# Pooled attention and two feed-forwards: the second output weight converted during the first feed-forward, and read back from DRAM

## The chip, the cores and the metric

One core of one Trainium2 chip. The metric is the device time of one execution in microseconds; of several executions the median is given. The profile is a trace of one execution. Its engines are TensorE (PE, with its weight loads as PEld), VectorE (DVE), ScalarE (ACT), GpSimd (POOL) and SyncE (SP); POOL and SP issue the transfers (DMA) between DRAM and the on-chip memory.

## What is computed

```python
k_p, v_p = k, v averaged over groups of 8 positions          # 576 -> 72
attn = softmax(q @ k_p.T / sqrt(64)) @ v_p                   # batch 8, 8 heads, 576 x 64
x = attn as 4608 tokens x 512
h = ((x @ w1) * (x @ w2)) @ w3                               # 512 -> 1024 -> 1024
x2 = h @ w_out                                               # 1024 -> 512
g = softplus(x2 @ w_in)                                      # 512 -> 2048
out = g @ w2_out                                             # 2048 -> 512, 4608 x 512
```

The attention inputs are 32-bit floats; the six weights arrive as 64-bit floats. `w2_out` (called `wo2_d` in the kernel, 2048 x 512) is the weight that the change is about.

## The kernel before

A 64-bit weight is loaded as pairs of 32-bit words and put together into 32-bit floats by one ACT operation and four DVE operations (`convert_1024`, lines 225 to 232: ABS of the upper word, a clamp, a shift, the sign, the lower word's top bits). Most matmuls take each operand as two numbers: hi, a copy rounded to the type that PE multiplies, and lo, what is left of it. The products hi·hi, hi·lo and lo·hi are summed (`mm3`, lines 122 to 124).

The program has two parts. In **the first**, 4608 tokens go in 9 blocks j of 512, and every block in 8 steps i (`p1_step`). A step multiplies x by 128 columns of w1 and of w2 (`ab`, 24 matmuls; ACT drains the first product at line 539, DVE multiplies at 542, ACT and DVE split the result at 117 and 118), and adds the step before to x2 (`x2_mm`, 12 matmuls). Attention for later tokens and weight conversions lie between the steps: `slot_1` calls `att_slot()` and then `bg(1)` or `bg(2)`, which runs one or two pieces of the generators in the list `background`. The last of these is `left_factors`, which converts `w_in`, forms the factors of a 7-product (Strassen-like) scheme and stores them in DRAM as hi and lo (`wis`), one of 8 tiles after another. x2 goes to DRAM too (`x2d`).

In **the second part**, 6 sweeps s of 768 tokens pass over 8 steps t each, so 48 steps n. A step makes 7 products (`product`, 42 matmuls of 384 columns into X and Z), with ACT draining at lines 802, 814, 820 and 837 and DVE adding at 807, 825 and 831. Softplus of the step before runs on ACT and DVE (`soft_ops`), and the step before that is multiplied by `w2_out` (`o_part`, 36 matmuls of 512 columns). The factors of a step come back from `wis` by DMAs that POOL issues (line 613), two a step, each after the product that reads its old place. Every engine runs its instructions in the order in which the code writes them.

`w2_out` is converted by `wo2_jobs`. Its places (tags `wgh0` to `wgl7`) are those of w1 and w2, so tile t can be written only when the last block no longer reads w1 and w2 there (`p1_done`). Tiles 0 to 3 are converted in pieces of 1024 columns during block j = 8, tiles 4 to 7 in pieces of 512 during steps 0 to 7 of the second part, by `bg(2)`, `bg(1)`, `bg(2)`, `bg(2)` in each step. The hi copy is line 640 (ACT), lo is 642 (DVE).

Of the kernel before, what the change touches and what calls it, by code (L numbers as in the profile page):

```python
# [8 lines left out]
F32 = mybir.dt.float32  # L9
F32R = mybir.dt.float32r  # L10
I32 = mybir.dt.int32
AF = mybir.ActivationFunctionType
# [36 lines left out]
def pooled_attention_two_ffn(ctx: ExitStack, tc: tile.TileContext, qT_d, kT_d, v_d, w12_d, w3T_d, wo_d, wi_d, wo2_d, out):  # L49
# [145 lines left out]


    background = []
    p1_done = set()

    def bg(steps):  # L200
        while steps and background:
# [21 lines left out]
    def convert_1024(raw, y):  # L223
        yi = y.bitcast(I32)
        nc.scalar.activation(y, raw[:, :, 1].bitcast(F32), AF.Abs, scale=HI_SCALE)
        yield
        nc.vector.tensor_scalar(y, y, HI_MIN, HI_MAX, op0=ALU.max, op1=ALU.min)
        nc.vector.tensor_scalar(yi, yi, 3, None, op0=ALU.logical_shift_left)
        yield
        nc.vector.scalar_tensor_tensor(yi, raw[:, :, 1], -0x80000000, yi, op0=ALU.bitwise_and, op1=ALU.bitwise_or)  # L230
        yield
        nc.vector.scalar_tensor_tensor(yi, raw[:, :, 0], 29, yi, op0=ALU.logical_shift_right, op1=ALU.bitwise_or)
        yield

    def left_factors():

        t2k_ring[0] = Ring([T2K + 8 + 2 * i for i in range(4)])
        stage = Ring([RAW + 8, RAW + 12])
        raw, y, S = mem(RAW, [P, 1024, 2], I32), mem(T2K, [P, 1024]), mem(T2K + 4, [P, 1024])
        for _ in range(8):  # L240
            yield
        nc.sync.dma_start(raw.rearrange("p n t -> p (n t)"), wi_d[0].rearrange("p q k f -> p (q k f)").bitcast(I32))
        yield
        for t in range(F8):
            yield from convert_1024(raw, y)
            if t + 1 < F8:
                nc.sync.dma_start(raw.rearrange("p n t -> p (n t)"), wi_d[t + 1].rearrange("p q k f -> p (q k f)").bitcast(I32))
            a11, a12, a22, a21 = (y[:, 256 * i:256 * i + 256] for i in range(4))
            s2, s3, s1, s4 = (S[:, 256 * i:256 * i + 256] for i in range(4))
            nc.vector.tensor_add(s1, a21, a22)  # L250
            nc.vector.tensor_sub(s3, a11, a21)
            yield
            nc.vector.tensor_sub(s2, s1, a11)
            nc.vector.tensor_sub(s4, a12, s2)
            yield
            w3_, w4_ = wis[t]
            for src, dsts in (
                (y[:, :512], [w3_[:, :, 0:2, :]]),
                (y[:, 512:768], [w4_[:, :, 2, :]]),
                (S[:, :512], [w3_[:, :, 2, :], w4_[:, :, 0, :]]),  # L260
                (S[:, 512:], [w4_[:, :, 1, :], w4_[:, :, 3, :]]),
            ):
                n = src.shape[1]
                st = stage([P, 2, 512])[:, :, :n]
                hi = st[:, 0, :].bitcast(F32R)
                nc.scalar.activation(hi, src, AF.Copy)
                yield
                nc.vector.tensor_sub(st[:, 1, :].bitcast(F32R), src, st[:, 0, :])
                n //= len(dsts)
                for i, dst in enumerate(dsts):  # L270
                    dst = dst.rearrange("p h c f -> p h (c f)") if len(dst.shape) == 4 else dst
                    nc.sync.dma_start(dst, st[:, :, n * i:n * i + n])
                yield


    ident = main.tile([P, P], F32, tag="ident", name="ident")
# [170 lines left out]
    with tc.manual_schedule():  # L447
# [115 lines left out]
        def p1_step(j, i, slots):  # L563
            st = ab(j, i)
            next(st)
            slots[0]()
            next(st)
            slots[1]()
            if (j, i) != (0, 0) and (j, i) <= (NB - 1, K1 // 2):
                x2_mm(*((j, i - 1) if i else (j - 1, K1 - 1)))  # L570
            slots[2]()
# [32 lines left out]

        c_ring = {0: Ring([0, 3]), 1: Ring([6])}
        e_ring, us = Ring([9, 12]), (mem(15, [P, TS]), mem(18, [P, TS]))
        o_ring = Ring([21, 23])
        wgroup = {}

        def load_factors(n, i):  # L610
# [3 lines left out]

        wo2_hl = {}

        def load_wo2(raw, t, parts):
            for n, i in enumerate(parts):
                f = t + F8 * i
                nc.sync.dma_start(raw[:, 512 * n:512 * n + 512, :].rearrange("p n t -> p (n t)"), wo2_d[f * P:f * P + P, :].bitcast(I32))  # L620

        def wo2_jobs(ts, ys, raws, parts):


            seq = [(t, p) for t in ts for p in parts]
            for n in range(min(len(raws), len(seq))):
                load_wo2(raws[n], *seq[n])
            for n, (t, p) in enumerate(seq):
                while (NB - 1, 2 * (t // 2) + 1) not in p1_done:
                    yield  # L630
                raw, y = raws[n % len(raws)], ys[n % len(ys)]
                yield from convert_1024(raw, y)
                if n + len(raws) < len(seq):
                    load_wo2(raw, *seq[n + len(raws)])
                if p[0] == 0:
                    w2 = [main.tile([P, 2, 512], F32R, tag=f"wg{x}{t}", name=f"w2{x}{t}") for x in "hl"]
                    for i in range(2):
                        wo2_hl[t + F8 * i] = w2[0][:, i, :], w2[1][:, i, :]
                hi, lo = (w[:, p[0]:p[-1] + 1, :].rearrange("p i f -> p (i f)") for w in w2)
                nc.scalar.activation(hi, y, AF.Copy)  # L640
                yield
                nc.vector.tensor_sub(lo, y, hi.bitcast(F32))
                yield


        xq_ring = Ring([XODD + 6 * i for i in range(8)] + [GBUF + 8])
# [40 lines left out]
        load_factors(1, 0)  # L687
        load_factors(1, 1)
        x2_load(0)
        background.append(wo2_jobs(range(4), [mem(T2K, [P, 1024]), mem(T2K + 4, [P, 1024])], [mem(RAW + 8 * i, [P, 1024, 2], I32) for i in range(2)], [(0, 1)]))  # L690

        for i in range(i7, K1):
            p1_step(NB - 2, i, [slot_1] * 3)
        xs = x2_steps(0)
        for i in range(K1):
            p1_step(NB - 1, i, [slot_1] * 3)
            p1_done.add((NB - 1, i))

            for _ in range((2, 1, 1, 0, 1, 1, 1, 0)[i]):
                next(xs)  # L700
        while background:
            bg(1)
        background.append(wo2_jobs(range(4, 8), [mem(25, [P, 512])], [mem(27, [P, 512, 2], I32)], [(0,), (1,)]))

        rest = [(i, ms) for i in range(K1 // 2, K1) for ms in ((0, 1), (2, 3))]

# [78 lines left out]
        for n in range(NH + 2):  # L785
            s, t = divmod(n, F8)
            h = n < NH
            if n == 2:

                o_ring = Ring([21, 23, 25, 27, 29])  # L790
            if h and t == 3 and s + 1 < NS:
                xs = x2_steps(s + 1)

            def factors(*when):

                if h and t in when and (s if t < 3 else s + 1) < NS:
                    next(xs, None)

            if h:
                soft[n, 0], soft[n, 1] = (c_ring[i]([P, TS]) for i in range(2))  # L800
                product(n, 0)
                nc.scalar.activation(snap[0], xz[0], AF.Copy)
            soft_step(n - 1, 0)
            soft_step(n - 1, 1)
            if h:
                product(n, 1)
                nc.vector.tensor_add(soft[n, 0][:, :HS], snap[0], xz[1])  # L807
            o_part(n - 2, 0, 0)
            factors(0, 7)
            soft_step(n - 1, 1)  # L810
            bg(2)
            if h:
                product(n, 2)
                nc.scalar.activation(snap[1], xz[0], AF.Copy)  # L814
            soft_step(n - 1, 0)
            o_part(n - 2, 0, 1)
            bg(1)
            if h:
                product(n, 3)
                nc.scalar.activation(snap[0], xz[1], AF.Copy)  # L820
            factors(0)
            soft_step(n - 1, 0)
            if h:
                product(n, 4)
                nc.vector.tensor_add(soft[n, 1][:, HS:], snap[0], xz[0])
            o_part(n - 2, 0, 2)
            factors(3, 4, 5, 6, 7)
            bg(2)
            if h:
                product(n, 5)  # L830
                nc.vector.tensor_add(soft[n, 1][:, :HS], snap[1], xz[1])  # L831
                soft_step(n, 1)
            o_part(n - 1, 1, 0)
            if h:
                soft_step(n, 1)
                product(n, 6)
                nc.scalar.activation(soft[n, 0][:, HS:], xz[0], AF.Copy)
                soft_step(n, 0)
            o_part(n - 1, 1, 1)
            soft_step(n, 1)  # L840
            soft_step(n, 0)
            o_part(n - 1, 1, 2)
            factors(7)
            bg(2)
            if h and t == 1 and s + 1 < NS:
                x2_load(s + 1)

# [53 lines left out]
```

## Time and profile before

| | |
|---|---|
| median of 3 runs | 1591.39 us (1590.06 to 1594.18) |
| the profiled execution, its own time | 1590.28 us |
| its span, first to last instruction | 1588.5 us |
| PE busy / PEld busy | 1527.4 us (96%) / 1280.6 us (81%) |
| DVE / ACT / POOL busy | 1003.4 us (63%) / 770.8 us (49%) / 125.5 us (8%) |

The span is what the trace covers; the 1.8 us between it and the execution's own time lie outside. Block j = 8 begins at 744.8 us, and the second part at 802.8 us. A wait in the trace is idle time of an engine just before an instruction, put down to what released it (after `<-`). Matmuls overlap in the trace, so an engine that is shown busy may still issue fewer of them.

### The profile page before, as it was taken

To read this page: it belongs to the slowest core of one execution; us is meant where nothing else is said; L and a number is where in the kernel's file an instruction comes from. 1 tells how busy PE (TensorE), PEld (TensorE's weight loads), DVE (VectorE), ACT (ScalarE), POOL (GpSimd) and SP (SyncE) were. 2 spreads that over 40 slices of the span, in tenths; PEclk is the share of its full clock that TensorE was granted. 3 is DMA by queue.
4 is the path that set the end of the run, shared out by engine and by line. 5 is a ranking of instruction groups with operands and counts; after the bars stand their busy time and mean duration, and the time that the engine had idled before them with its cause. 6 is when DMAs were issued, how large, how long until landed. Compare 5 with 4: busy or idle time off the path is not lost.

```text
span 1588.5 us, 20070 instructions
## 1 busy us (share of the span) xinstructions
PE 1527.4 (96%) x7712; PEld 1280.6 (81%) x7712; DVE 1003.4 (63%) x1526; ACT 770.8 (49%) x1611; POOL 125.5 (8%) x250
## 2 busy tenths in 40 slices
PE   4899999999999999999999999999999999999998
PEld 2457788888888888778877878989898988889897
DVE  7886666555533434322677777777677677768665
ACT  3445344444433333331355566565556566556554
POOL 3200111010100000000000000000000000000000
PEclk9999999999999999999999999999999999999999
DMA  8653245345411120005135435435335334434431
GB/s 280 204 182 112 71 165 158 125 149 169 132 42 63 51 63 29 12 16 197 69 114 179 157 112 182 130 115 197 120 113 194 118 119 158 155 114 133 145 112 40
DMA packets 64287, 198.44 MB, mean 125 GB/s; under 512 B 6336, under 2 KB 25792, under 8 KB 57024
## 3 DMA queue, kind: packets, MB, share of 16 engines
q0 software_dynamic: 22048, 116.40, 23.0%
q1 hardware_dynamic: 42144, 80.75, 14.9%
q8 instruction: 61, 1.00, 0.3%
q14 instruction: 34, 0.28, 0.1%
HBM read 163.58 MB, written 33.55 MB: 124 GB/s over the span
## 4 chain that ended last, share of the span: by engine, by line
PE 82%; DVE 10%; ACT 5%; DMA 2%; issue 1%; POOL 0%; SPq 0%; DVEq 0%; ACTq 0%; POOLq 0%
PE ab L122 8%; PE ab L124 8%; PE ab L123 8%; PE o L766 7%; PE o L765 7%; PE o L764 7%; PE x2p L122 4%; PE x2p L124 4%; PE x2p L123 4%; PE X L122 4%; PE X L123 4%; PE X L124 4%; PE Z L123 3%; PE Z L122 3%; PE Z L124 3%; PE pv L376 2%
## 5 line engine op out<-in xcount | busy, mean ns | idle before, releaser
L117 ACT ACTIVATE area_r<-area_f 128x768 fp32r<-128x768 f32 (+1 forms) x168 | 126.7, 754 | 241.0 <-DVE area_f L542 191.0
L766 PE MATMUL o<-w2h,area_r 128*128 128x512 f32 x576 | 228.1, 396 | 0.3 <-DVE area_r L118 0.3
L765 PE MATMUL o<-w2l,area_r 128*128 128x512 f32 x576 | 227.2, 394 | 0.0
L764 PE MATMUL o<-w2h,area_r 128*128 128x512 f32 x576 | 224.0, 389 | 0.0
L118 DVE TENSOR_TENSOR area_r<-area_f,area_r 128x768 fp32r<-128x768 f32 (+1 forms) x168 | 141.6, 843 | 111.6 <-ACT area_r L117 111.3
L122 PE MATMUL X<-area_r,wf 128*128 128x384 f32 x384 | 130.5, 340 | 9.8 <-ACT snap L814 3.3
L733 ACT ACTIVATE area_f<-area_f 128x768 f32<-128x768 f32 x96 | 81.3, 847 | 118.6 <-DVE area_f L831 116.9
L123 PE MATMUL X<-area_r,wf 128*128 128x384 f32 x384 | 129.6, 337 | 0.0
L737 DVE TENSOR_SCALAR area_f<-area_f 128x768 f32<-128x768 f32 x96 | 53.8, 560 | 119.8 <-ACT area_f L734 119.8
L124 PE MATMUL X<-area_r,wf 128*128 128x384 f32 x384 | 129.3, 337 | 0.0
L766 PEld LDWEIGHTS o<-w2h,area_r 128*128 128x128 f32 x576 | 108.0, 187 | 23.6 <-DVE area_r L118 0.7
L341 ACT ACTIVATE pr<-sc,mx 128x72 f32<-128x72 f32 x288 | 87.9, 332 | 77.0 <-DVE mx L339 77.0
L764 PEld LDWEIGHTS o<-w2h,area_r 128*128 128x128 f32 x576 | 108.2, 188 | 16.0 <-ACT area_r L117 0.3
L613 POOL DMA_DIRECT2D wf<-wis x96 | 51.6, 537 | 877.2 <-PE X L124 760.5
L765 PEld LDWEIGHTS o<-w2l,area_r 128*128 128x128 f32 x576 | 108.0, 187 | 15.8
L542 DVE TENSOR_TENSOR area_f<-area_f,ab 128x512 f32<-128x512 f32 x72 | 49.4, 686 | 110.0 <-PE ab L124 108.2
L122 PE MATMUL x2p<-area_r 128*128 128x512 f32 x288 | 116.1, 403 | 0.0
L124 PE MATMUL x2p<-area_r 128*128 128x512 f32 x288 | 112.9, 392 | 0.0
L123 PE MATMUL x2p<-area_r 128*128 128x512 f32 x288 | 112.6, 391 | 0.0
L122 PE MATMUL Z<-area_r,wf 128*128 128x384 f32 x288 | 96.9, 337 | 2.9 <-DVE area_f L807 2.9
L123 PE MATMUL Z<-area_r,wf 128*128 128x384 f32 x288 | 96.8, 336 | 0.0
L743 DVE TENSOR_TENSOR area_f<-area_f 128x768 f32<-128x768 f32 x96 | 92.0, 958 | 6.9 <-DVE area_f L742 0.5
(165 smaller groups left out, 3317.1 us busy)
## 6 DMA issues: line engine op xcount, KB each, us to landing
wf<-wis POOLq DMA_DIRECT2D x48, 1024.0 KB, 5.2
wf<-wis POOLq DMA_DIRECT2D x48, 768.0 KB, 4.6
area_f<-in_wo_dram SPq DMA_DIRECT2D x24, 512.0 KB, 4.1
wis<-area_f SPq DMA_DIRECT2D x40, 256.0 KB, 2.7
kv<-in_kT_dram POOLq DMA_DIRECT2D x32, 288.0 KB, 3.5
q<-in_qT_dram POOLq DMA_DIRECT2D x18, 512.0 KB, 4.5
kv<-in_v_dram POOLq DMA_DIRECT2D x32, 288.0 KB, 4.1
x2d<-area_f SPq DMA_DIRECT2D x36, 256.0 KB, 3.2
```

The source lines that it names most:

```text
L117: nc.scalar.activation(hi, src, AF.Copy)
L118: nc.vector.tensor_sub(lo, src, hi.bitcast(F32))
L122: nc.tensor.matmul(ps, whi, xhi, start=first, stop=False, skip_group_check=resumed)
L123: nc.tensor.matmul(ps, whi, xlo, start=False, stop=False, skip_group_check=resumed)
L124: nc.tensor.matmul(ps, wlo, xhi, start=False, stop=last, skip_group_check=resumed)
L341: nc.scalar.activation(pr[:, h, :], sc[h // 4][:, h % 4, :], AF.Exp, bias=mx[:, h:h + 1], scale=SCALE, accum_out=sm[:, h:h + 1])
L733: nc.scalar.activation(e, c, AF.Abs)
L737: nc.vector.tensor_scalar(u, e, 1.0, None, op0=ALU.add)
L743: nc.vector.tensor_add(c, c, u)
L764: nc.tensor.matmul(oacc[s][i], hl[:, 0, ts], wh, start=first, stop=False)
L765: nc.tensor.matmul(oacc[s][i], hl[:, 0, ts], wl, start=False, stop=False)
L766: nc.tensor.matmul(oacc[s][i], hl[:, 1, ts], wh, start=False, stop=last)
```

## The change

`w2_out` is converted in `left_factors`, after the last tile of `w_in`: for each of 8 tiles t, `convert_1024`, and then two halves of 512 columns, each split into hi (ACT) and lo (DVE) and stored to a new DRAM tile `w2s[t]`. The 64-bit rows are loaded by `load_raw_wo2`, one tile ahead. In block j = 8, after each second step, POOL issues the DMAs that bring hi and lo of two tiles into the places of w1 and w2 (`load_wo2`). `wo2_jobs`, its calls of `bg` in the second part and `p1_done` are gone, and `o_ring` has its five places from the start.

```diff
@@ left_factors
+    w2s = [dram.tile([P, 2, 2, 512], F32, name=f"w2s{t}", tag=f"w2s{t}") for t in range(F8)]
...
             if t + 1 < F8:
                 nc.sync.dma_start(raw.rearrange("p n t -> p (n t)"), wi_d[t + 1].rearrange("p q k f -> p (q k f)").bitcast(I32))
+            else:
+                load_raw_wo2(raw, 0)
...
+        for t in range(F8):
+            yield from convert_1024(raw, y)
+            if t + 1 < F8:
+                load_raw_wo2(raw, t + 1)
+            for i in range(2):
+                src = y[:, 512 * i:512 * i + 512]
+                st = stage([P, 2, 512])
+                nc.scalar.activation(st[:, 0, :].bitcast(F32R), src, AF.Copy)
+                yield
+                nc.vector.tensor_sub(st[:, 1, :].bitcast(F32R), src, st[:, 0, :])
+                nc.sync.dma_start(w2s[t][:, :, i, :], st)
+                yield
+
+    def load_raw_wo2(raw, t):
+        for i in range(2):
+            f = t + F8 * i
+            nc.sync.dma_start(raw[:, 512 * i:512 * i + 512, :].rearrange("p n t -> p (n t)"), wo2_d[f * P:f * P + P, :].bitcast(I32))
@@ the places and the jobs of the second part
-        o_ring = Ring([21, 23])
+        o_ring = Ring([21, 23, 25, 27, 29])
...
-        def wo2_jobs(ts, ys, raws, parts):
...
+        def load_wo2(t):
+
+            w2 = [main.tile([P, 2, 512], F32R, tag=f"wg{x}{t}", name=f"w2{x}{t}") for x in "hl"]
+            for n in range(2):
+                nc.gpsimd.dma_start(w2[n], w2s[t][:, n].bitcast(F32R))
+            for i in range(2):
+                wo2_hl[t + F8 * i] = w2[0][:, i, :], w2[1][:, i, :]
@@ block j = 8
-        background.append(wo2_jobs(range(4), ...
         for i in range(K1):
             p1_step(NB - 1, i, [slot_1] * 3)
-            p1_done.add((NB - 1, i))
+            if i % 2:
+                load_wo2(i - 1)
+                load_wo2(i)
...
-        while background:
-            bg(1)
-        background.append(wo2_jobs(range(4, 8), ...
@@ each step n of the second part
-            bg(2)
-            bg(1)
-            bg(2)
-            bg(2)
```

PE's instructions stand in the same order before and after. On the other engines three places matter. **ACT where the first part ends and the second begins.** `ab` is a product of the last two steps of block 8 (line 539 before, 560 after), `xr` the x2 of the first sweep that is split at line 117, `snap` the drain of step 0's first product. Before:

```order
L539 ACTIVATE area_f<-ab_6_0_5843 128x512
L225 ACTIVATE area_f<-area_f 128x1024
L117 ACTIVATE area_r<-area_f 128x512
L640 ACTIVATE w2h_5878<-area_f 128x1024
L117 ACTIVATE area_r<-xr_5406 128x768
L539 ACTIVATE area_f<-ab_7_0_5883 128x512
L117 ACTIVATE area_r<-area_f 128x512
L802 ACTIVATE snap_5409<-X 128x384
L117 ACTIVATE area_r<-xr_5406 128x768
L225 ACTIVATE area_f<-area_f 128x512
```

and now:

```order
L560 ACTIVATE area_f<-ab_6_0_5944 128x512
L117 ACTIVATE area_r<-area_f 128x512
L117 ACTIVATE area_r<-xr_5518 128x768
L560 ACTIVATE area_f<-ab_7_0_5976 128x512
L117 ACTIVATE area_r<-area_f 128x512
L799 ACTIVATE snap_5521<-X 128x384
L117 ACTIVATE area_r<-xr_5518 128x768
```

The conversion's ABS (225) and hi copy (640) no longer stand between the drains. **DVE in the first part**, at the step where the first tile of `w2_out` is converted. `vb` is the pooling of v, `x2p` the drain of a finished block, `pv` the attention output, `mx` softmax's maximum. Before:

```order
L558 COPY area_f<-x2p_1_2781 128x512
L558 COPY area_f<-x2p_3_2783 128x512
L118 TENSOR_TENSOR area_r<-pv_3372,area_r 128x4x128
L315 TENSOR_REDUCE vb_3321<-kv_1_1_3193 72x128
L542 TENSOR_TENSOR area_f<-area_f,ab_1_1_3386 128x512
```

and now:

```order
L579 COPY area_f<-x2p_1_2789 128x512
L579 COPY area_f<-x2p_3_2791 128x512
L226 TENSOR_SCALAR area_f<-area_f 128x1024
L227 TENSOR_SCALAR area_f<-area_f 128x1024
L229 SCALAR_TENSOR_TENSOR area_f<-area_f 128x1024
L118 TENSOR_TENSOR area_r<-pv_3386,area_r 128x4x128
L336 TENSOR_REDUCE vb_3331<-kv_1_1_3203 72x128
L231 SCALAR_TENSOR_TENSOR area_f<-area_f 128x1024
L563 TENSOR_TENSOR area_f<-area_f,ab_1_1_3401 128x512
```

The clamp, the shift, the sign and the low bits (lines 226 to 231 of the changed kernel) now stand ahead of the split of the attention output and of `ab`'s product; two subtractions of 512 columns follow for each tile. **POOL at the end of block 8**, between the factor loads of steps 0 and 1 and those of step 2. Now:

```order
L642 DMA w2h_6006<-w2s_102 128x1024
L642 DMA w2l_6007<-w2s_102 128x1024
L642 DMA w2h_6010<-w2s_103 128x1024
L642 DMA w2l_6011<-w2s_103 128x1024
L634 DMA wf<-wis_3_84 128x1536
L634 DMA wf<-wis_4_85 128x2048
```

These are the last four of 16 loads of 512 KB that stand ahead of step 2's factors (`wis_3_84`, `wis_4_85`) on POOL's queue; before, nothing stood between.

## Rows read from the trace of the kernel before

**Rows 1.** Windows: us, busy time (instructions) by engine, PEclk, DMA share, GB/s.

```profile
205.00:430.00 225.00, 225.00 (x1213) 185.00 (x1214) 136.63 (x242) 99.73 (x314) 24.88 (x50) 1.00 0.43 141
445.00:575.00 130.00, 130.00 (x718) 106.55 (x718) 45.63 (x83) 44.73 (x148) 8.16 (x20) 1.00 0.15 44
722.00:796.00 74.00, 74.00 (x328) 61.28 (x327) 33.73 (x42) 20.91 (x30) 0.00 (x0) 1.00 0.35 130
796.20:802.80 6.60, 6.28 (x26) 4.54 (x25) 5.67 (x8) 2.28 (x4) 0.00 (x0) 1.00 0.00 0
802.80:961.00 158.20, 145.50 (x698) 125.56 (x697) 120.34 (x169) 91.22 (x135) 9.54 (x18) 0.99 0.45 143
961.00:1101.70 140.70, 140.70 (x703) 126.60 (x702) 103.43 (x135) 85.24 (x123) 9.76 (x18) 1.00 0.48 157
809.40:812.70 3.30, 3.30 (x10) 3.01 (x10) 3.06 (x6) 1.68 (x3) 0.53 (x1) 0.50 0.00 0
```

**Rows 2.** Timeline of PE: first product of step 0 and of step 9.

```profile
802.83 0.33 PE L122 MATMUL X<-area_r,wf 128*128 128x384 f32 x1
...
960.96 0.33 PE L122 MATMUL X<-area_r,wf 128*128 128x384 f32 x1
```

**Rows 3.** Timeline of POOL: first factor load of step 9 and of step 10.

```profile
966.07 0.53 POOL L613 DMA_DIRECT2D wf<-wis  x1 [6.76 <-PE X L124]
...
981.71 0.53 POOL L613 DMA_DIRECT2D wf<-wis  x1 [6.77 <-PE X L124]
```

**Rows 4.** Waits of PE, 802.8 to 961 us: total, times, longest.

```profile
PE X L122 <- ACT snap L814: 3.3, 2, 1.7
PE X L122 <- ACT snap L802: 3.1, 2, 2.8
```

**Rows 5.** Timeline around the first stall of step 0: ACT, DVE, PE.

```profile
803.72 1.06 ACT L640 ACTIVATE w2h<-area_f 128x1024 fp32r<-128x1024 f32 x1 [3.15 <-DVE area_f L232]
...
808.27 0.63 ACT L117 ACTIVATE area_r<-area_f 128x512 fp32r<-128x512 f32 x1 [2.27 <-DVE area_f L542]
808.81 0.47 ACT L802 ACTIVATE snap<-X 128x384 f32<-128x384 f32 x1
...
806.42 1.22 DVE L642 TENSOR_TENSOR w2l<-area_f,w2h 128x1024 fp32r<-128x1024 f32 x1
807.56 0.68 DVE L542 TENSOR_TENSOR area_f<-area_f,ab 128x512 f32<-128x512 f32 x1
...
809.33 0.69 PE L122 MATMUL X<-area_r,wf 128*128 128x384 f32 x1 [2.85 <-ACT snap L802]
```

**Rows 6.** Groups by line and shape, 764 to 931 us, DVE and ACT.

```profile
L642 DVE TENSOR_TENSOR w2l<-area_f,w2h 128x512 fp32r<-128x512 f32 x8 | 5.5, 685 | 0.7 <-ACT w2h L640 0.7
L232 DVE SCALAR_TENSOR_TENSOR area_f<-area_f 128x1024 int32<-128x1024 int32 x4 | 4.9, 1224 | 0.1
L227 DVE TENSOR_SCALAR area_f<-area_f 128x1024 f32<-128x1024 f32 x4 | 2.8, 692 | 3.8 <-ACT area_f L225 3.8
L640 ACT ACTIVATE w2h<-area_f 128x512 fp32r<-128x512 f32 x8 | 5.0, 627 | 9.8 <-DVE area_f L232 9.8
L225 ACT ACTIVATE area_f<-area_f 128x1024 f32<-128x1024 f32 x4 | 4.5, 1124 | 0.0
```

**Rows 7.** Tile in_wi_dram: durations, first and last start; time to landing.

```profile
L247 SPq DMA_DIRECT2D area_f<-in_wi_dram x7: 328/338/342, 196.5 to 377.8; - x7
...
DMA to landing us min/median/max: 4.8/4.9/5.5
```

**Rows 8.** Tiles w2l and wis: durations, first and last start.

```profile
L642 DVE TENSOR_TENSOR w2l<-area_f,w2h x12: 681/686/1224, 775.2 to 929.9; 128x512 fp32r<-128x512 f32 x8, 128x1024 fp32r<-128x1024 f32 x4
...
L272 SPq DMA_DIRECT2D wis<-area_f x48: 512/519/1333, 205.4 to 429.6; - x48
```

**Rows 9.** DMA issues: KB each, median us to landing.

```profile
wf<-wis POOLq DMA_DIRECT2D x48, 1024.0 KB, 5.2
area_f<-in_wo_dram SPq DMA_DIRECT2D x24, 512.0 KB, 4.1
```

More of the change, by code (lines that the diff above doesn't have):

```diff
@@ L197, in pooled_attention_two_ffn @@
     background = []
-    p1_done = set()
     def bg(steps):
@@ L615, in pooled_attention_two_ffn @@
         wo2_hl = {}
[L617 to L620, printed above, removed]
-        def wo2_jobs(ts, ys, raws, parts):
[L625 to L643, printed above, removed]
+        def load_wo2(t):
[4 more added lines that the diff above has]
+                wo2_hl[t + F8 * i] = w2[0][:, i, :], w2[1][:, i, :]
         xq_ring = Ring([XODD + 6 * i for i in range(8)] + [GBUF + 8])
@@ L689, in pooled_attention_two_ffn @@
         x2_load(0)
-        background.append(wo2_jobs(range(4), [mem(T2K, [P, 1024]), mem(T2K + 4, [P, 1024])], [mem(RAW + 8 * i, [P, 1024, 2], I32) for i in range(2)], [(0, 1)]))
         for i in range(i7, K1):
             p1_step(NB - 2, i, [slot_1] * 3)
+        while background:
+            bg(1)
         xs = x2_steps(0)
@@ L696, in pooled_attention_two_ffn @@
             p1_step(NB - 1, i, [slot_1] * 3)
-            p1_done.add((NB - 1, i))
+            if i % 2:
+                load_wo2(i - 1)
+                load_wo2(i)
             for _ in range((2, 1, 1, 0, 1, 1, 1, 0)[i]):
                 next(xs)
-        while background:
-            bg(1)
-        background.append(wo2_jobs(range(4, 8), [mem(25, [P, 512])], [mem(27, [P, 512, 2], I32)], [(0,), (1,)]))
         rest = [(i, ms) for i in range(K1 // 2, K1) for ms in ((0, 1), (2, 3))]
@@ L787, in pooled_attention_two_ffn @@
             h = n < NH
-            if n == 2:
-                o_ring = Ring([21, 23, 25, 27, 29])
             if h and t == 3 and s + 1 < NS:
```

## The prediction, made before the changed kernel was run

> **What bounds the kernel now.** I read the windows first, because the change moves work between two stages and the whole span hides both. In the first part PE is busy for all of 205 to 430 us, all of 445 to 575 us and all of 722 to 796 us [rows 1]. From 961 to 1101.7 us, in the second part, it is busy for all 140.70 us too. Between these lies the only stretch that the change empties: 796.2 to 961 us, where PE has idle time.
>
> How long that stretch should be follows from the steps. Step 0 starts its first product at 802.83 us and step 9 at 960.96 us, so nine steps took 158.13 us [rows 2]. From step 9 to step 10 the same factor load moves by 981.71 − 966.07 = 15.64 us [rows 3], and the window from 961 us has nine such steps, 140.70 us [rows 1]. A step of 15.64 us is what PE needs when it waits for nothing. The first nine steps are therefore 158.13 − 9 × 15.64 = 17.4 us too long. They also hold six matmuls of 512 columns fewer: step 0 and step 1 have eight remainders of block 8's x2 in place of `o_part`, and six groups fit in step 0, so step 1 has two groups of six and three of `o_part`, 30 matmuls where a later step has 36. At 74.00 us for 328 matmuls of 512 columns [rows 1] one takes 0.226 us, so six are 1.4 us, and the loss is 18.7 us.
>
> The last two products of block 8 lose a little as well: in 796.2 to 802.8 us 25 matmuls begin, which need 25 × 0.226 = 5.6 of the 6.6 us [rows 1]. I call it 0.9 us. In all some 19.6 us are lost around the start of the second part.
>
> The waits say who is late. PE waits for ACT's drains of X, lines 814 and 802, 3.3 and 3.1 us [rows 4]; none of these instructions is slow by itself. The longest single wait shows how it comes about [rows 5]. The hi copy at 803.72 us stood 3.15 us in ACT's queue until DVE had put the weight together. Behind it ACT's drains came late; DVE's lo subtraction at 806.42 us stood ahead of the product at 807.56 us; ACT split that at 808.27 us and drained X only at 808.81 us. PE started at 809.33 us after 2.85 us of idling. From 809.4 to 812.7 us the granted clock was 0.50, the 1.2 GHz level [rows 1]; that is within the 19.6 us and no further term.
>
> One point decides how large the gain is. PE was shown idle for only 158.20 − 145.50 = 12.7 us of those nine steps, but its weight loads were busy 125.56 us in 158.20 us against 126.60 us in 140.70 us [rows 1]: at the later rate the same loads take 139.5 us, so 18.7 us are lost. I take 18.7 us. The Trainium skill, "Perfetto Trace Analysis", section "Identifying the Most-Contended Engine", says that the busy share of matmuls is a poor measure because they are pipelined, and that the busy share of weight loads is a good one. By its measure the sum has 18.7 us, by the matmuls' idle time 12.7 us; the count of steps agrees with the weight loads.
>
> **Removed from the boundary.** Each 512-column job there put three DVE operations of about 0.69 us and two of half the 1024-column 0.69 us on DVE, and two on ACT of 0.63 us or more [rows 6]; that is 2.8 us of DVE in six pieces, and with seven pieces a step some 3.2 us. The undisturbed step uses 103.43 / 9 = 11.5 us of DVE [rows 1]. Sum 14.7 of 15.64 us: DVE still fits on average, but its in-order queue no longer has room to answer PE in time. Without the jobs each step is like those from 961 us, which carry the same softplus, the same drains and the same splits of the next sweep's x2, and lose nothing. So the whole 19.6 us could go. I keep 0.7 us, one drain of 0.68 us [rows 5], because steps 0 and 1 also drain the last four sums of block 8, which no later step does. The bounds are 0 (the drains fit in free time) and 6.6 us (that only the 12.7 us of idle time and part of the entry come back, 19.6 − 13.0). Gain 18.9 us.
>
> **Added in the first part.** Per tile DVE gets 2 × 0.69 + 2 × 1.22 + 2 × 0.685 = 5.2 us, ACT 1.12 + 2 × 0.63 = 2.4 us [rows 6]; eight tiles are 42 us and 19 us. Where do they lie? `w_in` had 14 pieces a tile, and six tiles passed from 196.5 to 377.8 us [rows 7]: 181.3 / 84 = 2.16 us a piece. The new 64 pieces take 138 us, from the last store of `wis` at 429.6 us [rows 8] to about 570 us. There DVE was busy 45.63 of 130 us, 35%; 42 us in 138 us add 30%, so 65%. During the tiles of `w_in` it was busy 136.63 of 225 us, 61%, with operations of the same 1024 columns, and PE was busy all 225.00 us; the rates of weight loads, 185.00 of 225 us and 106.55 of 130 us, are both 82% [rows 1]. That cover is what hides the work: I cost it at nothing. The bounds are 0 (a gain is excluded, since PE is never idle there) and, if each tile's two 1.22 us operations and its 1.12 us ABS all reach PE, 8 × 3.6 = 28 us. The nearest row, the tiles of `w_in`, is at zero.
>
> One thing is tighter than with `w_in`. A tile's rows are loaded four pieces before ABS reads them, 8.6 us, where `w_in` had ten. Landing took 4.9 us, at most 5.5 us, for the same 1024 KB [rows 7], and two loads of 512 KB land in 4.1 us each [rows 9]. SP issues them right after DVE has read the old rows, and its x2 stores stand behind that for less than one piece. Cost nothing.
>
> **Added at block 8.** POOL gets 16 loads of 512 KB, four after each second step, each waiting for the products that read the old weights. Behind them on POOL stand only the factor loads. The last four are free to start near 802 us, when PE begins step 0; at 5.2 us for 1024 KB [rows 9] the 2 MB have landed by 813 us, and step 2's first factors 4 to 5 us after their own issue, by 818 us. Step 2 reads them near 802 + 15.6 + 14.3 = 832 us. Tile 7 itself is wanted in step 8. Nothing is late; it costs nothing, and the old loads of the raw rows, 16 of 512 KB, leave the same stretch.
>
> **Sum.** 1590.28 − 18.7 − 0.9 + 0.7 = 1571.4 us for an execution like the profiled one. That one was 1.1 us below the median of its three, so I forecast 1572.5 us.
>
> **The rivals.**
> - *Part of the loss belongs to the first sweep itself* (0.09). The last conversion was at 929.9 us [rows 8], within step 7, yet the lost time is spread over the nine steps; drains of block 8 and the filling of softplus are special to them. Then only PE's shown idle time of 12.7 us and 0.3 us of the entry return: 1590.28 − 13.0 + 1.1 = 1578.4 us. Against it: the next sweep change lies in the window from 961 us and loses nothing [rows 1].
> - *The conversions stall the first part* (0.08). A long DVE or ACT operation stands ahead of softmax or of `ab`'s drain, or the raw rows land late, and PE waits in 430 to 570 us. At half of the 28 us above it is 1586.5 us; slower from 19 us, or 2.4 us a tile, and with all of it 1600.5 us. For it: shorter notice for the loads, 65% of DVE. Against it: PE's full windows beside `w_in`.
> - *Slower, through POOL's queue* (0.02). The 16 loads hold up step 2's factors. It decides if they land after 832 us, 14 us later than reckoned; then every microsecond is PE's, so 19 us of it lose the gain (1591.5 us) and 24 us show as slower. It would need landings about four times those of [rows 9]. The Trainium skill, "SBUF — State Buffer", section "SBUF: two separate sides", warns that DVE operations in a two-port mode keep GpSimd from writing its descriptors, so that such loads wait. By that rule the loads would start late while DVE works; the trace shows no such wait for the factor loads: 0.53 us each on POOL [rows 3] while DVE is busy 74% of the time [rows 1].
> - *No effect* (0.03): the stalls move to another cause and the steps stay as long, 1591 us.
>
> **Chances and range.** The forecast has 0.78: within it 1569.5 us (all 19.6 us gone, no offset to the median, a microsecond of spread) to 1575 us. The range reaches to 1580 us, which takes in the first rival and the lighter part of the second. A change of 0.3%, 4.8 us, is about what can be told from none here. Faster: 0.78 + 0.09 + 0.06 of the second rival = 0.93; same: 0.04 (no effect, and 0.01 of the second); slower: 0.03.
>
> **What would show it.** Right: steps 0 to 9 in about 140 us, with step 1 the shortest; no wait of PE over 1 us for lines that answer to 802 and 814; no half clock at the start of the second part; weight loads at 82% in 430 to 570 us, DVE near 65%; the second part starting at the same time or 1 us earlier, near 802 us. Wrong: PE idle in 430 to 570 us, ACT waiting for the raw rows of `w2_out`, PE waiting for `wf` or `w2h`, or steps 0 to 2 still two or more microseconds too long.

## The result and the profile after

The changed kernel takes 1572.89 us (median of 4 runs, 1572.10 to 1573.79), the kernel before 1592.79 us (median of 4, 1590.06 to 1595.35). The ratio is 0.9878, 95% interval 0.9864 to 0.9891: 1.2% faster, 0.4 us from the forecast of 1572.5 us. The profiled execution took 1573.79 us, its span was 1572.0 us.

First the windows of the changed kernel's trace, in the columns of [rows 1]. The fourth is the entry into the second part (the last two products of block 8), the fifth is steps 0 to 8, from the first product of step 0 to that of step 9.

```profile
205.00:430.00 225.00, 224.98 (x1215) 184.89 (x1215) 136.20 (x242) 100.49 (x315) 25.35 (x50) 1.00 0.45 148
445.00:575.00 130.00, 129.23 (x704) 106.02 (x703) 81.01 (x129) 60.20 (x182) 12.71 (x21) 1.00 0.49 165
722.00:796.00 74.00, 74.00 (x328) 61.26 (x327) 20.13 (x28) 14.54 (x24) 7.94 (x15) 1.00 0.45 154
794.19:805.07 10.88, 10.88 (x49) 9.01 (x48) 4.68 (x6) 3.93 (x6) 2.11 (x4) 1.00 0.62 194
805.07:944.45 139.38, 139.38 (x697) 125.52 (x696) 97.18 (x126) 80.24 (x116) 11.02 (x20) 1.00 0.44 145
640.00:722.00 82.00, 74.55 (x425) 59.84 (x424) 24.50 (x52) 30.03 (x111) 0.54 (x1) 1.00 0.04 13
74.00:94.00 20.00, 15.25 (x51) 7.54 (x51) 17.01 (x32) 9.03 (x28) 4.76 (x10) 0.83 0.86 272
```

The nine steps that took 158.13 us [rows 2] take 139.38 us, 18.75 us less, and PE is busy for every microsecond of them. Its weight loads take 125.52 us, as before (125.56) [rows 1]: the same loads, closer together. DVE fell from 120.34 to 97.18 us and ACT from 91.22 to 80.24 us. The granted clock is 1.00 throughout, and from 794 to 945 us the list of PE's waits is empty, so that [rows 4] has no counterpart.

In 445 to 575 us the conversions have raised DVE from 45.63 to 81.01 us, 62%. PE now idles 0.77 us there, where it was busy for all 130.00 us.

The timeline of PE in the changed kernel shows the ends of the steps, and where block 0 begins (`ab`):

```profile
109.66 0.80 PE L122 MATMUL ab<-area_r,w_0h 128*128 128x512 f32 x1
...
805.07 0.33 PE L122 MATMUL X<-area_r,wf 128*128 128x384 f32 x1
...
944.45 0.33 PE L122 MATMUL X<-area_r,wf 128*128 128x384 f32 x1
```

Step 0 starts at 805.07 us, not at 802.83 [rows 2]. That lag comes from the start-up: the first `ab` product starts at 109.66 us here and at 106.17 us in the profile of before, of which two rows more are shown here, from the windows and from PE's timeline:

```profile
74.00:94.00 20.00, 16.32 (x59) 7.76 (x60) 16.78 (x32) 9.27 (x28) 4.80 (x11) 1.00 0.88 278
```

```profile
106.17 0.79 PE L122 MATMUL ab<-area_r,w_0h 128*128 128x512 f32 x1
```

In that start-up stretch the clock was 1.00 in the one profile of before, but 0.83 in that of the changed kernel. All 13 profiles of changed kernels in this study have 3.4 to 9.4 us at the 1.2 GHz level there and start block 0 at 107 to 113 us. This is the main reason why the profiled spans differ by 16.5 us only, while the nine steps and the entry alone give back more: 18.75 + 0.95 = 19.7 us (the entry took 11.83 us with the old jobs, below, and 10.88 us now). From the 19.7 us go 3.5 us of later start and 1.0 us in one step of the first part (experiment 1); 1.3 us come back in block 0, which from its first `ab` product to that of block 1 took 81.0 us here, 82.3 us before and 81.0 to 84.0 us in the other profiles, so this varies from run to run. That leaves 16.5 us. The medians differ by 19.9 us.

POOL's timeline of the changed kernel shows the last loads of hi and lo at block 8 and the factor loads behind them:

```profile
802.70 0.53 POOL L642 DMA_DIRECT2D w2h<-w2s  x1 [7.05 <-PE ab L124]
...
806.00 0.53 POOL L642 DMA_DIRECT2D w2l<-w2s  x1
810.18 0.53 POOL L634 DMA_DIRECT2D wf<-wis  x1 [3.66 <-PE X L124]
818.52 0.54 POOL L634 DMA_DIRECT2D wf<-wis  x1 [7.81 <-PE X L124]
```

The factor loads of step 2 wait for their places (products of X), not for the loads ahead of them. They are read from 835 us on, so the queue has time to spare.

### The profile page after: what moved, and what is told of

It is laid out like the page before. It is cut to its first block, busy times and chain, and to the rows that moved or that the text cites. A ratio compares the mean times of both kernels' runs of the same rounds, so it can differ in the third digit from the quotient of the medians.

```text
span 1572.0 us, 20121 instructions
## 1 busy us (share of the span) xinstructions
PE 1525.3 (97%) x7712; PEld 1283.2 (82%) x7712; DVE 1002.8 (64%) x1514; ACT 769.4 (49%) x1611; POOL 138.6 (9%) x266
## 3 DMA queue, kind: packets, MB, share of 16 engines
q1 hardware_dynamic: 46496, 89.14, 16.5%
## 4 chain that ended last, share of the span: by engine, by line
PE 91%; DVE 4%; ACT 2%; DMA 2%; issue 1%; POOL 0%; SPq 0%; DVEq 0%; ACTq 0%; POOLq 0%
PE o L766 8%; PE o L765 8%; PE ab L122 8%; PE o L764 8%; PE ab L124 8%; PE ab L123 8%; PE X L123 4%; PE X L124 4%; PE X L122 4%; PE x2p L122 4%; PE x2p L124 4%; PE x2p L123 4%; PE Z L123 3%; PE Z L122 3%; PE Z L124 3%; PE pv L397 2%
## 6 DMA issues: line engine op xcount, KB each, us to landing
area_f<-in_wo_dram SPq DMA_DIRECT2D x24, 512.0 KB, 4.3
q<-in_qT_dram POOLq DMA_DIRECT2D x18, 512.0 KB, 5.0
```

## The experiments

Twelve kernels were run. All times below are of runs beside the kernel before on one chip; "nine steps" is the time from the first product of step 0 to that of step 9, from each kernel's own profile.

**1. No conversion at all.** The tiles are not converted in the first part, and block 8 loads stored `w_in` in their place, so the second feed-forward's output is another one. This prices everything that the change adds in the first part.

```diff
-            else:
-                load_raw_wo2(raw, 0)
...
-        for t in range(F8):
+        for t in range(0):
             yield from convert_1024(raw, y)
...
-                nc.gpsimd.dma_start(w2[n], w2s[t][:, n].bitcast(F32R))
+                nc.gpsimd.dma_start(w2[n], wis[t][1][:, n].rearrange(...).bitcast(F32R))
```

> The changed kernel with the conversion of w2_out left out altogether: the loads of block 8 bring factors of w_in (wis) into the same places instead, so the output is another one. It prices what the change added to the first part. My theory (the added work lies under a busy PE): about 1.0 us less than the changed kernel, 1572 us, namely the one wait at 520 us where an x2 store landed late; PE busy all of 430 to 585 us. Rival (the 64 pieces slow the first part in many small ways that the gain outweighs): 5 us or more faster, 1568 us or less.

Measured: 1574.43 us (1572.30 to 1575.34), ratio 0.9875 (0.9853 to 0.9896), the same as the changed kernel within the intervals. Its window over the conversions' stretch:

```profile
445.00:575.00 130.00, 130.00 (x714) 106.60 (x714) 45.63 (x83) 45.83 (x160) 8.69 (x21) 1.00 0.15 47
```

Against 129.23 us of PE and 106.02 us of weight loads in the changed kernel, PE is full here. The conversion, with 35 us of DVE, costs PE 0.77 us of idle time, or, by the weight loads (0.58 us at 82%), 0.7 us. By the steps it is 1.0 us, all in one: the step near 513 us takes 11.58 us in the changed kernel and 10.57 us here and in the kernel before. It takes 11.2 to 11.6 us in all nine profiles that have the whole conversion and four places for the stage, so this small cost is not chance; experiment 9 finds its cause. Its nine steps take 139.38 us, from 803.96 to 943.34 us.

**2. and 3. One half of the old jobs each.** In the first kernel tiles 0 to 3 are converted by the old jobs at block 8 and tiles 4 to 7 in the first part. In the second tiles 0 to 3 are converted in the first part and tiles 4 to 7 by the old jobs in the second part, with two places of `o_ring` until step 2.

```diff
-        for t in range(F8):
+        for t in range(4, F8):
...
+        background.append(wo2_jobs(range(4), ...
...
-            if i % 2:
+            p1_done.add((NB - 1, i))
+            if i in (5, 7):
                 load_wo2(i - 1)
                 load_wo2(i)
```

```diff
-        for t in range(F8):
+        for t in range(4):
...
-        o_ring = Ring([21, 23, 25, 27, 29])
+        o_ring = Ring([21, 23])
...
+            if i in (1, 3):
                 load_wo2(i - 1)
                 load_wo2(i)
...
+        background.append(wo2_jobs(range(4, 8), ...
...
+            bg(2)
...
+            bg(1)
...
+            bg(2)
...
+            bg(2)
```

> Half of the change: tiles 0 to 3 of w2_out are converted in block 8 as before, tiles 4 to 7 in the first part and read back. Theory (the loss sits in the steps in which conversions stand in DVE's and ACT's queues): the entry loses 0.9 us again and step 0 some 2 to 5 us, steps 2 to 8 take 15.64 us; 1576 to 1579 us. Rival (the first sweep loses time by itself, or the halves only hurt together): steps 2 to 8 lose 3 us or more, or nothing at all is lost, 1573 us.

> The other half: tiles 0 to 3 are converted in the first part and read back, tiles 4 to 7 are converted in steps 0 to 7 of the second part as before. Theory: the entry and the first product of step 0 lose nothing, steps 1 to 8 lose 12 to 14 us; 1585 to 1588 us, and with the half of block 8 it adds up to the 19 to 20 us of the whole change. Rival (the lag comes from block 8 and only persists in the second part): under 6 us lost, 1579 us or less.

Measured: with the jobs of block 8 1578.29 us (1576.15 to 1579.44), ratio 0.9899 (0.9878 to 0.9921); with those of the second part 1588.69 us (1586.20 to 1595.23, 10 runs), ratio 0.9970 (0.9955 to 0.9985). The kernel with the jobs of block 8, its windows (entry, nine steps) and then its longest wait of PE at the boundary:

```profile
793.85:805.68 11.83, 11.50 (x49) 8.85 (x48) 8.81 (x11) 4.59 (x6) 2.12 (x4) 1.00 0.60 184
805.68:949.71 144.03, 141.20 (x698) 126.69 (x697) 99.99 (x129) 82.53 (x119) 11.00 (x20) 0.99 0.43 140
```

```profile
PE X L122 <- ACT snap L834: 2.8, 1, 2.8
```

The kernel with the jobs of the second part, its window of the nine steps and PE's waits:

```profile
805.64:959.68 154.04, 145.06 (x698) 125.65 (x696) 117.65 (x166) 89.00 (x132) 9.52 (x18) 0.99 0.44 143
```

```profile
PE X L122 <- ACT snap L846: 3.3, 2, 1.7
PE Z L122 <- DVE area_f L839: 2.4, 4, 0.9
```

The jobs of block 8 lose 0.95 us at the entry and 4.65 us in step 0, which takes 20.29 us instead of 15.64. The one long wait of [rows 5], 2.85 us, is there again with 2.83 us, and behind it, as in [rows 1], a stretch of 3.4 us at granted clock 0.50, which by an estimate costs half of its length, 1.7 us. The two make up 4.5 of the 4.65 us. The jobs of the second part lose nothing at the entry (10.88 us) and 14.66 us in the nine steps, spread over steps 1 to 8. Step 8 loses 1.2 us although the last piece ends in step 7, as it does in the kernel before. Step 3 is the longest (19.99 us); PE's longest wait stands in it, with the clock behind it:

```profile
863.70 0.47 PE L122 MATMUL X<-area_r,wf 128*128 128x384 f32 x1 [1.73 <-ACT snap L846]
```

```profile
863.98:867.39 3.41, 3.41 (x11) 3.02 (x11) 3.10 (x5) 2.31 (x4) 0.00 (x0) 0.50 0.35 132
```

Together 5.6 + 14.7 = 20.3 us, against the 19.7 us that the whole change returned: the parts add up, with 0.6 us left over.

**4. The loads behind block 8.** All 16 loads stand after the loop over block 8's steps instead of inside it.

```diff
             p1_step(NB - 1, i, [slot_1] * 3)
-            if i % 2:
-                load_wo2(i - 1)
-                load_wo2(i)
...
+        for t in range(F8):
+            load_wo2(t)
```

> The changed kernel with all 16 loads of w2_out behind block 8 instead of four after each second step. It prices the rival on POOL's queue. If the loads of one queue land in their order: 8 MB at 5.2 us for 1 MB keep the queue until 847 to 850 us, step 2's factors land near 853 us where they are read near 835 us, and the kernel loses 15 to 20 us, 1588 to 1593 us. If the factor load passes the weights or shares with them evenly: under 5 us lost, 1573 to 1578 us.

Measured: 1576.36 us (1573.24 to 1577.05), ratio 0.9884 (0.9857 to 0.9910), nine steps 139.40 us. The experiment does not test what it was meant to. POOL had nothing else to do between the old and the new place, so its order stayed and the loads started as soon as their products were done, as in the changed kernel. It is a repeat of that kernel and tells nothing about late loads; experiment 8 does.

**5. and 6. DVE's share alone, and ACT's share alone.** The changed kernel gets, in the second part, a job with only the DVE operations of eight 512-column conversions, on scratch places, and in the other kernel only the ACT operations. The calls of `bg` stand where they stood before the change, so that a step runs up to seven pieces. Nothing is left out; the results of the added operations are not used.

```diff
+        def extra_jobs():
...
+            for _ in range(8):
+                yield
+                nc.vector.tensor_scalar(y, y, HI_MIN, HI_MAX, op0=ALU.max, op1=ALU.min)
+                nc.vector.tensor_scalar(yi, yi, 3, None, op0=ALU.logical_shift_left)
...
+                nc.vector.tensor_sub(y, y, y)
+                yield
...
+        background.append(extra_jobs())
```

```diff
+            for _ in range(8):
+                nc.scalar.activation(y, raw[:, :, 1].bitcast(F32), AF.Abs, scale=HI_SCALE)
+                yield
...
+                nc.scalar.activation(y, y, AF.Copy)
+                yield
```

> The changed kernel with useless extra work in steps 0 to 7 of the second part: the five DVE operations of a 512-column conversion, eight times, at the places where the kernel before had them, on scratch data, without the two ACT operations. Theory (a full DVE queue answers PE late): steps 0 to 7 together 8 us or more longer than in the changed kernel (139.4 us for nine steps there, 14.7 us more with the whole jobs), 1581 us or more. Rival (ACT stands waiting for DVE in the middle of a job, and that holds up its drains; DVE's own time is small): under 4 us longer, 1577 us or less.

> The counterpart: only the two ACT operations of each 512-column conversion (the ABS and the hi copy), eight times at the old places, on scratch data, without DVE's five. Theory: nine steps within 2 us of the changed kernel's 139.4 us, 1573 to 1575 us. Rival (ACT's operations push the drains back by themselves): 4 us or more.

Measured: DVE's operations 1585.94 us (1583.44 to 1586.65), ratio 0.9961 (0.9946 to 0.9975); ACT's 1572.30 us (1571.90 to 1573.58), ratio 0.9881 (0.9864 to 0.9897). DVE's operations alone, window of the nine steps and PE's waits:

```profile
806.22:957.65 151.43, 143.80 (x698) 124.20 (x696) 117.91 (x167) 79.90 (x116) 10.58 (x20) 1.00 0.41 133
```

```profile
PE X L122 <- ACT area_f L858: 3.6, 4, 1.6
PE Z L122 <- DVE area_f L828: 2.0, 3, 0.9
```

ACT's operations alone, the same window:

```profile
803.61:942.98 139.37, 139.37 (x698) 125.58 (x697) 97.19 (x126) 88.65 (x132) 11.01 (x20) 1.00 0.44 145
```

ACT carries as much as with the whole jobs (88.65 us against 89.00) and PE loses nothing. DVE at 117.91 us, 78% of the stretch, makes PE lose 12.05 us. So 12 of the 14.7 us of the second part are DVE's alone, although PE's largest wait names ACT: ACT has no work added here and can be late only through DVE, as in [rows 5]. Of the remaining 2.6 us some 1.7 us go with the clock: the 3.4 us at granted clock 0.50 in step 3 of experiment 3 have no counterpart in the nine steps here (granted clock 1.00). The rest was not taken apart. The jobs of block 8 had no such pair of experiments; that DVE is behind their wait as well is read from [rows 5] alone.

**7. Twice the conversion in the first part.** The eight tiles are converted a second time after the first, until 723 us.

```diff
-        for t in range(F8):
+        for n in range(2 * F8):
+            t = n % F8
...
```

> The changed kernel with every tile of w2_out loaded, converted and stored twice in the first part: 64 more pieces, until about 700 us, so across the dense end of the attention, too. It asks how much cover is left. Theory: PE stays busy up to 640 us apart from single waits of 1 us for late x2 stores; in 640 to 720 us, where PE waits for softmax anyway, the pieces cost 2 to 6 us; 1574 to 1579 us. Rival (the first part was just full): 10 us or more, 1583 us or over.

Measured: 1574.53 us (1572.60 to 1575.56), ratio 0.9892 (0.9877 to 0.9907). The expected loss of 2 to 6 us in 640 to 722 us did not come. Its windows:

```profile
640.00:722.00 82.00, 74.56 (x426) 59.92 (x425) 44.11 (x76) 38.32 (x124) 0.48 (x1) 1.00 0.29 104
805.15:944.52 139.37, 139.37 (x697) 125.59 (x696) 97.15 (x126) 80.23 (x116) 11.02 (x20) 1.00 0.44 145
```

PE idles in 640 to 722 us anyhow (74.55 us busy of 82 in the changed kernel), and 20 us more of DVE do not add to it: the 7.4 us have another cause. The median is 2.2 us above that of experiment 6 on the same chip, with overlapping ranges and intervals; the profile has no place for such a loss.

**8. The loads in step 0.** All 16 loads start only after step 0's first factor load, on the same queue.

```diff
             p1_step(NB - 1, i, [slot_1] * 3)
-            if i % 2:
-                load_wo2(i - 1)
-                load_wo2(i)
...
+                if n == 0:
+                    for w in range(F8):
+                        load_wo2(w)
```

> All 16 loads of w2_out in step 0, on POOL's queue behind the first factor load of step 2 and ahead of its second. In the kernel with the loads behind block 8 nothing else stood on POOL's queue between the old and the new place, so the loads started as early as before and its 1576 us say nothing of the queue; this one moves them past a factor load. If one queue lands in its order: 8 MB keep it from 812 to 855 us, step 2's second factors, read near 840 us, land near 858 us, and 10 to 20 us are lost: 1583 to 1593 us. If the factors share with the weights or pass them: under 5 us, 1573 to 1578 us.

Measured: 1579.14 us (1574.71 to 1582.05), ratio 0.9920 (0.9897 to 0.9943). Its windows (nine steps, and the clock behind the stall), POOL's timeline, and PE's at step 2:

```profile
808.03:952.72 144.69, 141.16 (x698) 127.09 (x697) 97.15 (x126) 80.26 (x116) 18.68 (x34) 0.99 0.54 185
847.40:850.80 3.40, 3.27 (x10) 3.30 (x11) 0.00 (x0) 0.97 (x2) 0.00 (x0) 0.50 1.07 402
```

```profile
813.76 0.53 POOL L642 DMA_DIRECT2D w2h<-w2s  x1
...
820.65 0.53 POOL L642 DMA_DIRECT2D w2l<-w2s  x1 [2.02 <-issue]
...
832.11 0.53 POOL L642 DMA_DIRECT2D w2l<-w2s  x1 [0.91 <-DMA w2h<-w2s]
834.00 0.54 POOL L634 DMA_DIRECT2D wf<-wis  x1 [1.37 <-DMA w2l<-w2s]
```

```profile
847.53 0.66 PE L122 MATMUL Z<-area_r,wf 128*128 128x384 f32 x1 [3.53 <-DMA wf<-wis]
```

The second factors of step 2 were issued at 834.00 us behind 8 MB of weights, and PE waited 3.53 us for them once, then ran 3.4 us at the 1.2 GHz level (granted clock 0.50). Only step 2 is longer, by 5.3 us: the wait and, by the same estimate as above, 1.7 us for the clock. So the queue does land in order and does hold up the factors when the loads are late, as the prediction's rival on POOL's queue and the first of the two recorded cases had it; the size, 10 to 20 us, was reckoned too high, because loads issued back to back moved 8 MB in 31 us, 3.9 us per MB, not 5.2.

**9. Six places for the stage.** The stage ring of the first part has four places of 2 KB while `w_in` is converted. `S` is no longer needed afterwards, so its two places can join.

```diff
+        t2k_ring[0] = Ring([T2K + 4 + 2 * i for i in range(6)])
         for t in range(F8):
             yield from convert_1024(raw, y)
```

> The changed kernel with six places instead of four for the drains of the first part while w2_out is converted (the area that the factors of w_in no longer need). Theory: the one step of 11.3 to 11.6 us near 513 us, where ACT waits for an x2 store before it may drain again, returns to 10.57 us; 1 us less in the trace, 1572 us, too little for the times to tell. Rival (the wait is not for the places but for the transfers themselves, or moves to the next step): the step stays or another grows.

Measured: 1572.78 us (1571.66 to 1574.68), ratio 0.9865 (0.9851 to 0.9880). Its window over the conversions' stretch:

```profile
445.00:575.00 130.00, 130.00 (x709) 106.54 (x707) 81.47 (x130) 60.24 (x182) 12.71 (x21) 1.00 0.48 166
```

This explains where the 0.77 us of PE in the first part go. The changed kernel's timeline of ACT, SP and PE near 513 us:

```profile
515.53 0.63 ACT L285 ACTIVATE area_f<-area_f 128x512 fp32r<-128x512 f32 x1
519.57 0.60 ACT L560 ACTIVATE area_f<-ab 128x512 f32<-128x512 f32 x1 [3.40 <-DMA x2d<-area_f]
...
512.00 0.81 SPq L294 DMA_DIRECT2D area_f<-in_wo_dram  x2
514.23 0.81 SPq L582 DMA_DIRECT2D x2d<-area_f  x2
...
521.43 0.39 PE L348 MATMUL sc<-kT,q 128*128 128x144 f32 x1 [0.77 <-DVE area_r L118]
```

ACT's drain of `ab` needed a place whose x2 store was still under way. SP had issued two raw loads of `w2_out` at 512.0 us and the store at 514.2 us; the store landed at 519.5 us, so ACT waited 3.40 us and PE in the end 0.77 us. Time to landing of the four x2 stores there, changed kernel, experiment 1 and six places:

```profile
DMA to landing us min/median/max: 5.2/5.5/6.5
...
DMA to landing us min/median/max: 2.6/2.8/3.4
...
DMA to landing us min/median/max: 4.9/5.3/6.0
```
The same drain of ACT without the conversion (experiment 1) and with six places:

```profile
516.18 0.60 ACT L558 ACTIVATE area_f<-ab 128x512 f32<-128x512 f32 x1 [2.17 <-PE ab L124]
```

```profile
516.54 0.60 ACT L561 ACTIVATE area_f<-ab 128x512 f32<-128x512 f32 x1
```

With six places the stores land as late as before, but ACT does not wait, PE is busy 130.00 of the 130 us from 445 us, and the step near 513 us takes 10.57 us, as in experiment 1, instead of 11.6. So the wait was for the place. That the stores land late goes with the conversion's transfers; which of these, the raw loads or the stores of hi and lo, was not tested. In the times this is not to be told apart from the changed kernel (next run): the ranges overlap.

**10. and 11. How many pieces a step can bear.** The DVE-only job of experiment 5 with four conversions instead of eight: in one kernel with up to four pieces a step, in the other with up to seven.

```diff
-            for _ in range(8):
+            for _ in range(4):
...
-            bg(2)
+            bg(1)
...
-            bg(2)
+            bg(1)
...
-            bg(2)
+            bg(1)
```

(The diff is against experiment 5 and is that of four pieces; with seven only the first edit is made.)

> DVE's operations of four 512-column conversions alone, as in the run with DVE's part of all eight, but four pieces a step instead of seven, over six steps. At seven pieces DVE's part cost 12.05 us for eight conversions. Theory (DVE has room until its queue is full): at four pieces DVE needs some 13.4 us of a step of 15.64 us and the four conversions cost under 1.5 us; nine steps take 139.4 to 140.9 us. Rival (every operation delays PE wherever it stands): half of 12.05 us, nine steps in 145.4 us.

> The same four conversions' DVE operations at seven pieces a step, in the first three and a half steps, as a control of the run with four pieces. Theory: the loss belongs to the steps that hold the pieces and to one or two behind them while DVE catches up: 4 to 7 us in steps 1 to 5, none from step 6; nine steps in 143 to 146 us. Rival (no room at any density, or a lag that persists): equal to the run with four pieces, or losses until step 8.

One run each: 1576.06 and 1578.18 us. Windows of the nine steps, four pieces and then seven:

```profile
805.96:947.06 141.10, 140.24 (x697) 125.27 (x696) 107.23 (x147) 80.32 (x116) 10.89 (x20) 1.00 0.43 143
```

```profile
806.56:949.18 142.62, 140.66 (x697) 125.17 (x696) 107.82 (x147) 80.18 (x116) 10.59 (x20) 1.00 0.43 141
```

The same work on DVE (107.2 and 107.8 us) costs 1.7 us spread out, just over what was expected, and 3.2 us when it is dense, under the 4 to 7 us expected. Spread out, the loss lies mostly in step 8 (16.78 us), although the last piece ends at 901 us, in step 6; why it shows there was not tested. Steps 0 and 2 to 5 take 15.64 us each. Dense, it lies in steps 1 to 3 (15.51, 16.55 and 16.53 us, where the changed kernel has 14.25, 15.64 and 15.64). So the density within a step matters, but four conversions at the front cost 3.2 us where eight cost 12.05 us: the four later ones cost the more. There, in steps 4 to 6 of experiment 5 (18.14, 18.09 and 17.68 us), the splits of the next sweep's x2 are on DVE too; that these are the reason was not tested.

**12. The changed kernel again.**

> The changed kernel once more, on the same chip as the kernel with six places, to compare their times: 1573 us, nine steps in 139.4 us, and the step near 513 us at 11.3 to 11.6 us again.

Measured: 1575.10 us (1572.72 to 1576.58) on the chip of experiment 9, where the kernel before took 1594.22 us (median of 7); ratio 0.9878 (0.9862 to 0.9895), as the first time. Nine steps: 139.36 us.

## Why the prediction was right, step by step

- **The loss of nine steps, 18.7 us.** Measured 18.75 us, all of it returned. The choice between 18.7 us and PE's shown idle time of 12.7 us was the decisive one, and it fell to the count of steps and the weight loads. The rule of the Trainium skill that the prediction cites ("Perfetto Trace Analysis", "Identifying the Most-Contended Engine") agrees with this trace: 18.7 us by the weight loads, 12.7 us by the matmuls' idle time, 18.75 us returned. Some 1.7 us of the gap between the two are the 3.3 us at granted clock 0.50 of [rows 1], in which PE counts as busy. The rival that the first sweep loses time by itself is out: without the jobs its steps take 15.64 us, step 1 14.25 us.
- **The entry, 0.9 us.** 0.95 us, and it belongs to the jobs of block 8 (experiment 2).
- **Kept for the drains of block 8, 0.7 us.** Nothing had to be kept: steps 0 and 1 have no wait, and step 1 takes 14.25 us, 1.4 us less than a full step, just the six matmuls reckoned.
- **The mechanism: DVE's in-order queue.** Shown by experiments 5 and 6: DVE's operations alone bring back 12 us of the second part's 14.7, ACT's none; the same operations spread thinner cost less (experiments 10 and 11, one run each), so it is their place in the queue and not their number alone. For the 5.6 us of block 8 the queue is read from [rows 5], not tested apart. Two things were coarser than the prediction had them. The jobs of block 8 bring a stall of their own, 4.65 us in step 0 with the fall of the clock, and the jobs of the second part do not cost the same in each step.
- **The first part, cost nothing.** DVE came to 62% (65% forecast), the last store was issued at 572.8 us (about 570 forecast) and weight loads stayed at 82%. But the cost is 0.7 to 1.0 us, not nothing. The sentence that failed is that SP's x2 stores stand behind the raw loads "for less than one piece. Cost nothing": in one step a store landed 5.2 us after its issue, where the same store took 2.6 us in the kernel before, and ACT's next drain waited for its place. What was left out is the landing beside the conversion's transfers, not SP's queue. Experiment 9 shows the cause, by taking away the need for that place.
- **POOL's queue.** Harmless as the loads were placed, and in the order reckoned; experiment 8 shows what it costs when they are late. In the changed kernel POOL issued each load in 0.53 to 0.54 us. The delay that the Trainium skill warns of ("SBUF — State Buffer", "SBUF: two separate sides") is shown by no run here; what held POOL between the loads of experiment 8 was not tested.
- **The start of the second part** was forecast near 802 us and was 805.07 us. The step that failed is taking the start-up of one profile as fixed. Whether the changed kernel itself starts later cannot be settled: there is only one profile of the kernel before, and its further runs range from 1589.82 to 1597.56 us, so that the profiled 1590.28 us lies at their low end. Their mean granted clock was 0.990 to 0.997 (0.996 in the profiled one, 0.993 in that of the changed kernel), so most of its runs, too, had less clock than the profiled one; in which stretch, no trace shows.
- **The total.** That 1572.89 us lies within 0.4 us of the forecast is in part luck. The 0.7 us kept needlessly stand against the 1.0 us that the first part was not to cost; the kernel before came out 1.4 us above the median that the forecast started from; and the changed kernel again took 1575.10 us (experiment 12). The mechanism and the 18.7 us are not luck.

## What to carry to other kernels

Where a loop repeats one step, count what a stretch lost from the start of one step to that of the next, beside an undisturbed one; the idle time shown for a pipelined engine was too small by a third here (12.7 of 18.75 us), in part because a slower clock counts as busy. An engine that answers another step by step is full well before its busy share says so: in the nine steps DVE at 70% cost PE nothing and at 76 to 78% between 1.7 and 14.7 us, by where the work lay; the same operations in the first part, at 62%, cost about 1 us, and that through a late store, not through DVE. When work is moved with its loads, look also at the small stores that share its queue, and at how many places wait for them.

## What the runs showed of the hardware that was not expected

- Sixteen loads of 512 KB issued back to back on one queue landed in order, 8 MB in 31 us (about 270 GB/s beside other traffic), while a lone load of 1 MB took 5.2 us [rows 9]. From the seventh load on POOL's issue itself stalled, up to 2.02 us between two loads.
- Beside the conversion's transfers, four 256 KB stores of x2 took 5.2 to 6.5 us to land; without them (experiment 1) the same four took 2.6 to 3.4 us.
- An idle time of PE of 3.53 us (experiment 8) was followed by 3.4 us at the 1.2 GHz level, as after the 2.85 us of [rows 5], the 2.83 us of experiment 2 and the 1.73 us of experiment 3; a step with such a stretch lost more than the wait (5.3 us for 3.53, 4.65 for 2.83).
